# From the block loop to the tail: tile-by-tile loads through POOL's queue, a pool of its own for grad_out, the last products by kind and w_down in pieces

## The chip, the cores and the metric

The kernel runs on one core of one Trainium2 chip, as one launch. The time is device microseconds (us) of one execution; times are given as the median of several runs, and one execution was also taken by the profiler. Smaller is better.

## The reference

It is the forward pass and all gradients of a block with an adaptive layer norm, a spectral mixer and a bilinear feed-forward, for 2048 tokens (S), width 576 (D) and hidden width 4608 (F), in bfloat16.

```python
def A_ref(x, w_r, w_i):                       # spectral mixer
    X = jnp.fft.rfft2(x.astype(jnp.float32), axes=(-2, -1))
    return jnp.fft.irfft2(X * (w_r + 1j * w_i), s=(S, D), axes=(-2, -1)).astype(jnp.bfloat16)

def B_ref(x, w_gate, w_up, w_down):           # bilinear feed-forward
    return ((x @ w_gate) * (x @ w_up)) @ w_down

def f(x, w_r, w_i, w_gate, w_up, w_down, c, w_mod):
    sa, ca, ga, sb, cb, gb = split6(silu(c) @ w_mod)
    h = layernorm(x) * (1 + ca) + sa
    x = x + ga * A_ref(h, w_r, w_i)
    h = layernorm(x) * (1 + cb) + sb
    return x + gb * B_ref(h, w_gate, w_up, w_down)

out, vjp = jax.vjp(f, x, w_r, w_i, w_gate, w_up, w_down, c, w_mod)
return (out, *vjp(grad_out))                  # eight gradients
```

## The kernel before

The 2048 tokens are 16 tiles of 128, the hidden width is 36 blocks of 128 (`fb`). The Fourier transforms are matmuls with tables that lie in DRAM. The work goes in four stretches: a head (the forward mixer and the start of the gradient of the hidden layer), the loop over the 36 blocks, the backward mixer (`t1`, then `t2`), and the last products (`t3`), with the output `x + gb * B`.

**The block loop** computes, for each `fb`, gate and up (`gup`, L620 and L625), their products with the hidden gradient (`hhT`, `ggT`, `guT`), the sum of the gradient that goes back to the tokens (`u8p`, matmuls of L654, added into `acc` by DVE at L659), and three weight gradients (`product(fb, 0..2)`, matmuls `u57p` of L572): 0 is `gon` (grad_out) by `hh_sf`, 1 is `h2p` by `gg_sf` and 2 is `h2p` by `gu_sf`. The `_sf` tiles are the block's tiles with tokens on the partitions, made by DMA transposes on SP's queue (L643). Each product is two groups (halves of the width) of 16 matmuls of 128x288, stored through `so` and, for 1 and 2, turned once more by DMA (`woT`, L583) before the store. `hhT` of every block is also stored to DRAM (`hhT_d`, L638, POOL's queue), since `t3` needs it in another layout.

**From loop to tail.** Behind the last block come 32 `u8p` outputs of four matmuls each, which finish `acc` tile by tile, and six products: those of block 34 (0, 1, 2) and of block 35 (0, 1, 2). Beside them runs `t1`, sixteen tiles through four steps: `t1_norm` (DVE and ACT: the gradient of the second layer norm, `gn`, `jk`, `ab`, `u`, `v`, and with grad_out `gxr`, `gyr`; L850 to L861), `t1_turn` (PE transposes `trp` L866, and column sums by matmul: `csA` from n2c, `csB`, `csC` from yc; L769), `t1_cols` (`zp`, L886, table RD) and `t1_rows` (`vp`, L894, table G1, result `b_Vp`). `t1_norm` loads `n2c` (the normed tokens), `goc` (grad_out) and `yc` (the mixer's output) for two tiles at a time, from SP's queue, in two buffers each (L835); it stores `gxr` per tile from POOL's queue (L860).

**t2** works through 19 chunks of frequencies and takes `wn` (the spectral weights, L917, one DMA on POOL's queue). **t3** computes `u3p` (L1113): for each of 16 tiles and two halves of the width 36 matmuls, `hl` (hidden rows, four DMAs of 9 blocks for every two tiles, L1099) by `wdA` (w_down's blocks 0 to 14) and `wdB` (blocks 15 to 35), both loaded by SP (L1088). t3's matmuls fill PE beside t2. Five of its tiles start a `section` that finishes a gradient of the modulation (`pr`, L803).

**What sets the order.** A scheduler places the instructions of every engine in one fixed order by priorities: work in `tc.high_priority(n)` is placed as if it stood n earlier in the program. `HEAD_START` (350) and `SPREAD` (40) give t1 and t2 that lead; the six products are what is placed last, as fill. `tc.issue_after(x)` keeps an instruction behind x on the same engine's queue; `behind(list)` does it for several. A queue issues in order: an instruction that waits holds up all behind it. A tile's buffer comes free when the last reader of the tile that had it is done, and a pool that is opened where another has been closed waits tile by tile for what lies there. Before, `wdB`'s one buffer lies over `hh_sf`, `gg_sf` and `gu_sf` of both last blocks.

Of the kernel before, what the change touches and what calls it, by code (L numbers as in the profile page):

```python
# [19 lines left out]
NT = 16  # L20
# [10 lines left out]
NCH = 19  # L31
HEAD_START = 350
SPREAD = 40


def _tables():
# [46 lines left out]
def build(ctx, tc, A_x, A_w_r, A_w_i, B_w_gate, B_w_up, B_w_down, c_in, w_mod, grad_out,  # L83
# [93 lines left out]
    res3cm = tc.tile_pool(name="res3", bufs=1, reuse_waits="tile")  # L177
    res3 = res3cm.__enter__()
    h2T = res3.tile([128, NT, 5, 128], BF, name="h2T")
    res2cm = tc.tile_pool(name="res2", bufs=1, reuse_waits="tile")  # L180
    res2 = res2cm.__enter__()
    h2p = res2.tile([128, NT, DP], BF, name="h2p")
    h2n = h2p[:, :, 0:D]
    gonf = res2.tile([128, NT * D + 64], BF, name="gon")
    gon = gonf[:, 0:NT * D].rearrange("p (t d) -> p t d", t=NT)

    with ExitStack() as hs:
        def pool(name, bufs, side="left", space=None, stack=hs):
# [332 lines left out]
    with ExitStack() as ms:  # L521
# [13 lines left out]
        with ExitStack() as bs:  # L535
# [99 lines left out]
            def turn_items(fb):  # L635
                def turns_():
                    hhT, ggT, guT = trip[fb][2:5]
                    nc.gpsimd.dma_start(hhT_d[:, :, fb, :].rearrange("tp f x -> f tp x"), hhT[:].rearrange("f (tp ti) p -> f tp (ti p)", ti=2))  # L638
                    sfs[fb] = []
                    for nm, srcT in (("hh_sf", hhT), ("gg_sf", ggT), ("gu_sf", guT)):  # L640
                        sf = sfp.tile([128, NT, 128], BF, name=nm)
                        with tc.high_priority(-2 * HEAD_START if fb == NFB - 1 else 0):
                            turned = nc.sync.dma_start_transpose(out=sf[:], in_=srcT[:].rearrange("f t p -> f (t p)"))  # L643
                        sfs[fb].append(sf)
                    if fb % FBT == 1 and fb + 3 < NFB:
                        wTs[fb // FBT + 1] = wT_load(fb + 3, [turned.ins] * 5)
                return turns_
# [49 lines left out]
                for h in range(2):  # L697
                    u8_output([NFB - 2, NFB - 1], t, h)
            fill.clear()
            for fb_ in (NFB - 2, NFB - 1):  # L700
                for i in range(3):
                    for f in product(fb_, i):
                        f()
        res2cm.__exit__(None, None, None)
        res3cm.__exit__(None, None, None)

    with ExitStack() as ts:
# [11 lines left out]
        tl0 = pool("tl0", 1)  # L721
        o2p = pool("o2p", 2)
        oAp = pool("oAp", 1)
        oBp = pool("oBp", 1)
        tl = pool("tl", 1)
        Vp = pool("vp", 1).tile([128, NG, 128], BF, name="b_Vp")
        tl3 = pool("tl3", 1)
# [90 lines left out]
        with ExitStack() as r1:  # L818
# [6 lines left out]
            with tc.high_priority(HEAD_START):  # L825
                for k in rings:
                    nc.vector.memset(rings[k][:, :, D:DP], 0.0)
            ld, gyTs, zts = {"order": []}, {}, {}

            def t1_norm(t):  # L830
                if t % 2 == 0:
                    for k, src in (("n2c", n2_d), ("goc", go_v), ("yc", y_d)):
                        ld[k] = c1.tile([128, 2, D], BF, name=k)
                        with behind(ld["order"]):
                            ins = nc.sync.dma_start(ld[k][:], src[:, t:t + 2, :])  # L835
                        if t == 4:
                            ld["after"] = ins.ins
                    if t < 4:
                        ld["order"] = [ins.ins]
                        with behind(ld["order"]):  # L840
                            for k, tag in ((("RD", "tA"),), (("G1", "tB"), ("BD2", None), ("BDA", None)))[t // 2]:
                                T[k] = load_table(tl0, k, tag)
                        ld["order"] = [tab_ins[k]]
                    ld[t // 2] = (ld["n2c"], ld["yc"])
                n2 = ld["n2c"][:, t % 2, :]
                gh, gx, gy = (rings[k][:, t % 3, 0:D] for k in ("ghr", "gxr", "gyr"))
                nc.scalar.copy(gh, acc(t))
                s12 = c1.tile([128, 2], FP32, name="s12")
                gn = c1.tile([128, D], BF, name="gn2")
                nc.vector.scalar_tensor_tensor(out=gn[:], in0=acc(t), scalar=1.0, in1=opcb_h[:], op0=MUL, op1=MUL, accum_out=s12[:, 0:1])  # L850
                jk = c1.tile([128, D], BF, name="jk2", bufs=1)
                nc.vector.scalar_tensor_tensor(out=jk[:], in0=gn[:], scalar=1.0, in1=n2, op0=MUL, op1=MUL, accum_out=s12[:, 1:2])
                ab = c1.tile([128, 2], FP32, name="ab2")
                nc.vector.tensor_scalar(out=ab[:], in0=s12[:], scalar1=-1.0 / D, scalar2=rstd2g[:, t:t + 1], op0=MUL, op1=MUL)
                u = c1.tile([128, D], BF, name="u2")
                nc.scalar.activation(out=u[:], in_=gn[:], func=ACT.Identity, bias=ab[:, 0:1], scale=rstd2g[:, t:t + 1])
                v = c1.tile([128, D], BF, name="v2", bufs=1)
                nc.vector.scalar_tensor_tensor(out=v[:], in0=n2, scalar=ab[:, 1:2], in1=u[:], op0=MUL, op1=ADD)
                nc.vector.tensor_tensor(out=gx, in0=v[:], in1=ld["goc"][:, t % 2, :], op=ADD)
                nc.gpsimd.dma_start(gx1_d[:, t, :], gx)  # L860
                nc.vector.tensor_tensor(out=gy, in0=gx, in1=ga_h[:], op=MUL)  # L861

            def t1_turn(t):
                pt = ps_fp.tile([128, 5, 128], BF, name="trp", tag="fp")
                for m in range(5):
                    nc.tensor.transpose(pt[:, m, :], rings["gyr"][:, t % 3, wide(m)], ident[:])  # L866
                gyTs[t] = c1.tile([128, 5, 128], BF, name="gyT")
                nc.scalar.copy(gyTs[t][:], pt[:])
                gh, gx = rings["ghr"][:, t % 3, :], rings["gxr"][:, t % 3, :]
                n2c, yc = ld[t // 2]  # L870
                if t == 0:
                    add_zero(csA, csB, csC, first=True)
                for h in range(2):
                    colsum(csB, h, gh[:, h * 288:(h + 1) * 288])
                diag(csA, csB, 288, gh, n2c[:, t % 2, :])
                diag(csC, csB, 352, gx, yc[:, t % 2, :])
                if t == NT - 1:
                    add_zero(csA, csB, csC, first=False)

# [23 lines left out]
            after = ld["after"]  # L903
# [10 lines left out]
        rA = ts  # L914
        ra = pool("ra", 1, "right", stack=rA)
        wn = ra.tile([128, 2, NT, FP], BF, name="wn2")
        nc.gpsimd.dma_start(wn[:].rearrange("k c a f -> k (c a f)"), wn_d)  # L917
        fg = pool("fg", 2, "right", stack=rA)
        rB = ExitStack()
        A_ = pool("rb", 1, "right", stack=rB).tile([128, 2, NT, FP], BF, name="j_A")  # L920
# [160 lines left out]

        csF = ps_cs.tile([128, 512], FP32, name="csF", tag="csB")
        wdA = oAp.tile([128, 15, D], BF, name="wdA")
        wdB = oBp.tile([128, NFB - 15, D], BF, name="wdB")

        def wd_load(dst, k, f0, n):
            with tc.issue_after(after):
                nc.sync.dma_start(dst[:, k:k + n, :], B_w_down[f0 * 128:(f0 + n) * 128, :].rearrange("(j f) d -> f j d", f=128))  # L1088

        wd_load(wdA, 0, 0, 8)  # L1090
        wd_load(wdA, 8, 8, 7)
        prs = {}
        for tp_ in range(NT // 2):
            hls = []
            for b0 in range(0, NFB, 9):
                nq = 4 * tp_ + b0 // 9
                hl = hlp.tile([128, 9, 256], BF, name="hl2") if nq >= 12 and (nq - 12) % 13 < 7 else o2p.tile([128, 9, 256], BF, name="hl", bufs=6)
                with tc.issue_after(after):
                    nc.sync.dma_start(hl[:], hhT_d[tp_, :, b0:b0 + 9, :])  # L1099
                hls.append(hl)  # L1100
                if tp_ == 0 and b0 in (9, 18):
                    wd_load(wdB, 10 * (b0 // 9 - 1), 15 + 10 * (b0 // 9 - 1), 9 + b0 // 9)
            x1t = o2p.tile([128, 2, D], BF, name="x1t3", bufs=1)
            nc.gpsimd.dma_start(x1t[:], x1_d[:, 2 * tp_:2 * tp_ + 2, :])
            got = o2p.tile([128, 2, D], BF, name="got3", bufs=1)
# [1 line left out]
            for ti in range(2):  # L1107
                t = 2 * tp_ + ti
                ob = o2p.tile([128, D], BF, name="ob3")
                for h in range(2):  # L1110
                    p2 = ps_u3.tile([128, 512], FP32, name="u3p")
                    for fb in range(NFB):
                        mm = nc.tensor.matmul(p2[:, 0:288], lhsT=hls[fb // 9][:, fb % 9, ti * 128:(ti + 1) * 128], rhs=(wdA[:, fb] if fb < 15 else wdB[:, fb - 15])[:, h * 288:(h + 1) * 288], start=(fb == 0), stop=(fb == NFB - 1))  # L1113
# [99 lines left out]
```

## Time and profile before

| | |
|---|---|
| median of 3 runs | 1591.95 us (1589.98 to 1597.13) |
| profiled execution | 1594.8 us, of which span 1593.0 us |
| mean granted clock of PE | 0.992 |
| busy | PE 1535.0, DVE 1045.6, ACT 559.8, POOL 170.3 us |
| bytes moved by DMA | 280.64 MB, mean 176 GB/s |
| n2c, 288 KB, issue to landing | 4.6 us (median of eight) |
| gx_d, 144 KB, from POOL's queue | 3.3 us (median of sixteen) |
| wn, 2336 KB, from POOL's queue | 10.3 us |
| wdB, 1440 and 1584 KB, from SP's queue | 7.6 and 18.8 us |

An engine is busy when it executes. Its waits are put down to what came last. PE is TensorE's matmuls, DVE VectorE, ACT ScalarE, POOL GpSimd, SP SyncE; POOLq and SPq are their DMA queues. A line such as "PE csA L769 <- DMA n2c<-n_d: 2.4, 3, 1.3" reads: PE's instruction that writes csA at line 769 waited for the DMA that fills n2c from n_d, 2.4 us in all, three times, 1.3 us at the longest. A row of windows has the window, its length, and for PE, weight loads, DVE, ACT and POOL the busy time with the number of instructions; then the granted clock, the share of time in which the 16 DMA engines were busy, and GB/s. A row of the chain has its start, its length and what it was.

### The profile page before, as it was taken

What the parts mean: (1) busy time and instruction counts of PE and PEld (TensorE: products, weight loads), DVE (VectorE), ACT (ScalarE), POOL (GpSimd) and SP (SyncE); (2) the same over time, 40 slices, a digit from 0 to 9 for tenths busy, and PEclk for the clock granted to TensorE, in tenths of its full rate; (3) what the DMA queues carried; (4) which work ended last, traced back from release to release, by engine and by line L of the source; (5) the groups of instructions that cost most, each with busy time, mean ns of one, the idle gap of its engine ahead of it and who ended that gap; (6) DMA issues with size and microseconds to landing.
All of it is one profiled execution on the core that took longest, in us unless ns stands there. A gap on an engine that the chain in (4) does not pass through costs nothing.

```text
span 1593.0 us, 30039 instructions
## 1 busy us (share of the span) xinstructions
PE 1535.0 (96%) x11370; PEld 1035.0 (65%) x11370; DVE 1045.6 (66%) x2626; ACT 559.8 (35%) x1108; POOL 170.3 (11%) x283
## 2 busy tenths in 40 slices
PE   6999989999999999999999999999999989899997
PEld 4666533567666666766666676666666666677775
DVE  6866763666666666666666666666666774678655
ACT  6666632322222222222222222222222365466022
POOL 0001212101010100101010010101000011100232
PEclk9999999999999999999999999999999999999998
DMA  9869998779877686786868686767857786635775
GB/s 319 275 194 237 242 259 228 166 139 143 141 152 150 130 177 104 158 152 134 162 130 144 140 171 118 164 133 129 180 103 143 191 264 197 218 112 179 286 224 159
DMA packets 485252, 280.64 MB, mean 176 GB/s; under 512 B 407633, under 2 KB 452434, under 8 KB 484210
## 3 DMA queue, kind: packets, MB, share of 16 engines
q1 hardware_dynamic: 459922, 185.65, 55.1%
q0 software_dynamic: 25184, 93.07, 19.8%
q8 instruction: 89, 1.46, 0.4%
q14 instruction: 57, 0.47, 0.1%
HBM read 108.77 MB, written 82.31 MB: 120 GB/s over the span
## 4 chain that ended last, share of the span: by engine, by line
PE 77%; DMA 9%; DVE 7%; issue 3%; ACT 2%; SPq 0%; POOL 0%; DVEq 0%; ACTq 0%; POOLq 0%
PE u57p L572 26%; PE u8p L654 17%; PE gup L625 16%; PE u4p L377 7%; PE gup L620 2%; DMA xc<-in_A_x_dram 2%; DMA n2c<-n_d 2%; DMA Xn<-xn_d 2%; DMA wmj<-in_w_mod_dram 1%; DMA wdB<-in_B_w_down_dram 1%; DVE pr L803 1%; PE u3p L1113 1%; PE yp L485 1%; PE yp L1022 1%; PE zp L315 1%
## 5 line engine op out<-in xcount | busy, mean ns | idle before, releaser
L659 DVE TENSOR_TENSOR acc<-acc,u8p 128x288 f32<-128x288 f32 x1088 | 489.2, 454 | 314.6 <-PE u8p L654 314.2
L654 PE MATMUL u8p<-wT,ggT 128*128 128x288 bf16 x1152 | 327.5, 286 | 2.1 <-DVE acc L659 2.1
L654 PE MATMUL u8p<-wT,guT 128*128 128x288 bf16 x1152 | 327.2, 286 | 0.0
L625 PE MATMUL gup<-h2T,wgu 128*128 128x512 bf16 x1152 | 294.9, 379 | 0.0
L575 ACT CAST so<-u57p 128x288 bf16<-128x288 f32 x216 | 86.0, 398 | 521.4 <-PE u57p L572 515.6
L572 PE MATMUL u57p<-gon,hh_sf 128*128 128x288 bf16 x1152 | 188.6, 286 | 0.4 <-DMA hh_sf<-hhT 0.4
L572 PE MATMUL u57p<-h2p,gg_sf 128*128 128x288 bf16 x1152 | 187.6, 286 | 0.0
L572 PE MATMUL u57p<-h2p,gu_sf 128*128 128x288 bf16 x1152 | 186.2, 286 | 0.0
L625 PEld LDWEIGHTS <-wgu 128*128 128x128 bf16 x1152 | 109.5, 98 | 98.8 <-issue 17.1
L654 PEld LDWEIGHTS <-ggT 128*128 128x128 bf16 x1152 | 112.6, 98 | 67.2 <-issue 14.0
L377 PE MATMUL u4p<-goT,wdT 128*128 128x512 bf16 x656 | 151.1, 379 | 4.4 <-DVE ghh_st L141 3.8
L654 PEld LDWEIGHTS <-guT 128*128 128x128 bf16 x1152 | 112.7, 98 | 56.2 <-issue 2.6
L1113 PEld LDWEIGHTS <-hl 128*128 128x128 bf16 x1152 | 111.5, 98 | 35.7 <-issue 7.5
L572 PEld LDWEIGHTS <-hh_sf 128*128 128x128 bf16 x1152 | 112.6, 98 | 29.0 <-DMA hh_sf<-hhT 0.7
L572 PEld LDWEIGHTS <-gu_sf 128*128 128x128 bf16 x1152 | 112.5, 98 | 28.4
L572 PEld LDWEIGHTS <-gg_sf 128*128 128x128 bf16 x1152 | 112.5, 98 | 28.3
L627 ACT CAST gT<-gup 128x512 bf16<-128x512 f32 x144 | 84.3, 585 | 130.4 <-PE gup L625 130.4
L377 PEld LDWEIGHTS <-wdT 128*128 128x128 bf16 x656 | 61.9, 98 | 77.2 <-issue 11.5
L627 ACT CAST uT<-gup 128x512 bf16<-128x512 f32 x144 | 84.3, 585 | 73.6 <-PE gup L625 73.6
L1113 PE MATMUL u3p<-wdB,hl 128*128 128x288 bf16 x672 | 94.8, 288 | 8.0 <-DMA wdB<-in_B_w_down_dram 7.0
L638 POOL DMA_DIRECT2D hhT_d<-hhT x36 | 33.2, 921 | 504.4 <-DVE hhT L629 475.4
L139 ACT CAST ghh_st<-u4p 128x512 bf16<-128x512 f32 x88 | 51.1, 585 | 68.1 <-PE u4p L377 67.7
(358 smaller groups left out, 1734.0 us busy)
## 6 DMA issues: line engine op xcount, KB each, us to landing
ghhT_d<-ghh_st POOLq DMA_DIRECT2D x36, 512.0 KB, 4.7
ghh<-ghhT_d POOLq DMA_DIRECT2D x36, 512.0 KB, 7.3
hhT_d<-hhT POOLq DMA_DIRECT2D x36, 512.0 KB, 6.6
hl<-hhT_d SPq DMA_DIRECT2D x32, 576.0 KB, 6.9
out_dram<-woT SPq DMA_DIRECT2D x72, 128.0 KB, 2.0
wdn<-in_B_w_down_dram SPq DMA_DIRECT2D x18, 288.0 KB, 4.3
out_dram<-so SPq DMA_DIRECT2D x36, 144.0 KB, 2.6
wgu<-in_B_w_gate_dram SPq DMA_DIRECT2D x18, 256.0 KB, 3.4
```

The source lines that it names most:

```text
L139: nc.scalar.copy(dst, src)
L315: mm = nc.tensor.matmul(zp[:, :FP], lhsT=hTs[t][:, m, :], rhs=T["RD"][:, m, cc, :], start=(m == 0), stop=(m == 4))
L377: nc.tensor.matmul(pt[:], lhsT=wdTs[k][:, j, m, :], rhs=goT[:, 4 * sb4:4 * sb4 + 4, m, :], start=(m == 0 and n == 5), stop=(m == n - 1))
L572: mm = nc.tensor.matmul(pw[0][:, 0:288], lhsT=sf[:, t, :], rhs=rhs_n[:, t, h * 288:(h + 1) * 288], start=(t == 0), stop=(t == NT - 1))
L575: nc.scalar.copy(so[:, h * 288:(h + 1) * 288], pw[0][:, 0:288])
L620: nc.tensor.matmul(pts[-1][:], lhsT=wgu[r, 8, jw * 128:(jw + 1) * 128], rhs=h2T[r, 4 * sb4:4 * sb4 + 4, 4, :], start=True, stop=False)
L625: nc.tensor.matmul(pts[k][:], lhsT=wgu[:, 4 * wi_ + m, jw * 128:(jw + 1) * 128], rhs=h2T[:, ts_, m, :], start=False, stop=(m == 3))
L627: nc.scalar.copy((gT, uT)[wi_][:, ts_, :], pts[k][:])
L638: nc.gpsimd.dma_start(hhT_d[:, :, fb, :].rearrange("tp f x -> f tp x"), hhT[:].rearrange("f (tp ti) p -> f tp (ti p)", ti=2))
L654: nc.tensor.matmul(pu[:, 0:288], lhsT=l_, rhs=r_, start=(k == 0), stop=(k == len(mms) - 1))
L659: nc.vector.tensor_tensor(out=dst, in0=dst, in1=pu[:, 0:288], op=ADD)
L1113: mm = nc.tensor.matmul(p2[:, 0:288], lhsT=hls[fb // 9][:, fb % 9, ti * 128:(ti + 1) * 128], rhs=(wdA[:, fb] if fb < 15 else wdB[:, fb - 1 ...
```

## The change

1. **grad_out in its own pool.** `gon` and `h2p` lay in one pool, `gon` above `h2p`. Now `gon` has a pool of its own below `h2p`'s, and each is given up by itself.
2. **Last products by kind.** The six run as 0 of 34, 0 of 35, 1 of 34, 1 of 35, 2 of 34, 2 of 35. The transpose that makes `hh_sf` of block 35 is no longer put late with the other two.
3. **t1's loads by tile.** `n2c`, `goc` and `yc` come one tile at a time (147,456 bytes instead of 294,912, the 288 KB of the profile's rows), in four buffers instead of two of double size, through POOL's queue instead of SP's. The chain that held them and the tables in one order is gone; the tables are asked for with tiles 0 and 1.
4. **wn in four pieces** on POOL's queue, behind the gx stores of tiles 7, 9, 11 and 13.
5. **w_down in pieces.** `wdA` comes in four DMAs on POOL's queue, behind the yc loads of tiles 4, 6, 8 and 10, instead of two on SP's. `wdB` becomes three pools of seven blocks, each loaded by two DMAs on SP's queue, between the first four `hl`. Those `hl` and the first four wdB pieces get the priority `AHEAD` (3000); `hl` is no longer held behind t1's loads.

```diff
+AHEAD = 3000
...
-    res2 = res2cm.__enter__()
-    h2p = res2.tile([128, NT, DP], BF, name="h2p")
-    gonf = res2.tile([128, NT * D + 64], BF, name="gon")
+    res2gcm = tc.tile_pool(name="res2g", bufs=1, reuse_waits="tile")
+    gonf = res2gcm.__enter__().tile([128, NT * D + 64], BF, name="gon")
+    res2cm = tc.tile_pool(name="res2", bufs=1, reuse_waits="tile")
+    h2p = res2cm.__enter__().tile([128, NT, DP], BF, name="h2p")
...
-                        with tc.high_priority(-2 * HEAD_START if fb == NFB - 1 else 0):
+                        with tc.high_priority(-2 * HEAD_START if fb == NFB - 1 and nm != "hh_sf" else 0):
...
-            for fb_ in (NFB - 2, NFB - 1):
-                for i in range(3):
+            for i in range(3):
+                for fb_ in (NFB - 2, NFB - 1):
                     for f in product(fb_, i):
                         f()
...
-        oBp = pool("oBp", 1)
+        oBps = [pool("oB%d" % k, 1) for k in range(3)]
...
-                if t % 2 == 0:
-                    for k, src in (("n2c", n2_d), ("goc", go_v), ("yc", y_d)):
-                        ld[k] = c1.tile([128, 2, D], BF, name=k)
-                        with behind(ld["order"]):
-                            ins = nc.sync.dma_start(ld[k][:], src[:, t:t + 2, :])
...
+                for k, src in (("n2c", n2_d), ("goc", go_v), ("yc", y_d)):
+                    ld[k] = c1.tile([128, D], BF, name=k, bufs=4)
+                    ins = nc.gpsimd.dma_start(ld[k][:], src[:, t, :])
+                ld["at", t] = ins.ins
+                for k, tag in {0: (("RD", "tA"),), 1: (("G1", "tB"), ("BD2", None), ("BDA", None))}.get(t, ()):
+                    with tc.issue_after(tab_ins["RD"]) if t else ExitStack():
+                        T[k] = load_table(tl0, k, tag)
...
-        nc.gpsimd.dma_start(wn[:].rearrange("k c a f -> k (c a f)"), wn_d)
+        for k in range(4):
+            with tc.issue_after(ld["gx", 7 + 2 * k]):
+                nc.gpsimd.dma_start(wn[:, k // 2, 8 * (k % 2):8 * (k % 2) + 8, :].rearrange("k a f -> k (a f)"), wn_d[:, k * 8 * FP:(k + 1) * 8 * FP])
...
-        wdB = oBp.tile([128, NFB - 15, D], BF, name="wdB")
-        wd_load(wdA, 0, 0, 8)
-        wd_load(wdA, 8, 8, 7)
+        wdBs = [oBps[k].tile([128, 7, D], BF, name="wdB%d" % k) for k in range(3)]
+        def wd_load(f0, n, t):
+            dst = wdA[:, f0:f0 + n, :] if f0 < 15 else wdBs[(f0 - 15) // 7][:, (f0 - 15) % 7:(f0 - 15) % 7 + n, :]
+            with tc.issue_after(ld["at", t]) if t < NT else ExitStack():
+                (nc.gpsimd if t < NT else nc.sync).dma_start(dst, B_w_down[f0 * 128:(f0 + n) * 128, :].rearrange("(j f) d -> f j d", f=128))
+        for k in range(4):
+            wd_load(4 * k, 3 if k == 3 else 4, 4 + 2 * k)
...
-                with tc.issue_after(after):
+                with tc.high_priority(AHEAD if tp_ == 0 else 0):
                     nc.sync.dma_start(hl[:], hhT_d[tp_, :, b0:b0 + 9, :])
...
-                if tp_ == 0 and b0 in (9, 18):
-                    wd_load(wdB, 10 * (b0 // 9 - 1), 15 + 10 * (b0 // 9 - 1), 9 + b0 // 9)
+                if tp_ == 0 and b0 < 27:
+                    f0 = 15 + 7 * (b0 // 9)
+                    with tc.high_priority(AHEAD if b0 < 18 else 0):
+                        wd_load(f0, 4, NT)
+                        wd_load(f0 + 4, 3, NT)
```

More of the change, by code (lines that the diff above doesn't have):

```diff
@@ L704, in build @@
         res2cm.__exit__(None, None, None)
+        res2gcm.__exit__(None, None, None)
         res3cm.__exit__(None, None, None)
@@ L827, in build @@
                     nc.vector.memset(rings[k][:, :, D:DP], 0.0)
-            ld, gyTs, zts = {"order": []}, {}, {}
+            ld, gyTs, zts = {}, {}, {}
             def t1_norm(t):
-                if t % 2 == 0:
-                    for k, src in (("n2c", n2_d), ("goc", go_v), ("yc", y_d)):
-                        ld[k] = c1.tile([128, 2, D], BF, name=k)
-                        with behind(ld["order"]):
-                            ins = nc.sync.dma_start(ld[k][:], src[:, t:t + 2, :])
[L836 to L845, printed above, removed]
+                for k, src in (("n2c", n2_d), ("goc", go_v), ("yc", y_d)):
+                    ld[k] = c1.tile([128, D], BF, name=k, bufs=4)
+                    ins = nc.gpsimd.dma_start(ld[k][:], src[:, t, :])
+                ld["at", t] = ins.ins
+                ld[t] = (ld["n2c"], ld["yc"])
+                for k, tag in {0: (("RD", "tA"),), 1: (("G1", "tB"), ("BD2", None), ("BDA", None))}.get(t, ()):
+                    with tc.issue_after(tab_ins["RD"]) if t else ExitStack():
+                        T[k] = load_table(tl0, k, tag)
+                n2 = ld["n2c"][:]
                 gh, gx, gy = (rings[k][:, t % 3, 0:D] for k in ("ghr", "gxr", "gyr"))
@@ L858, in t1_norm @@
                 nc.vector.scalar_tensor_tensor(out=v[:], in0=n2, scalar=ab[:, 1:2], in1=u[:], op0=MUL, op1=ADD)
-                nc.vector.tensor_tensor(out=gx, in0=v[:], in1=ld["goc"][:, t % 2, :], op=ADD)
-                nc.gpsimd.dma_start(gx1_d[:, t, :], gx)
+                nc.vector.tensor_tensor(out=gx, in0=v[:], in1=ld["goc"][:], op=ADD)
+                ld["gx", t] = nc.gpsimd.dma_start(gx1_d[:, t, :], gx).ins
                 nc.vector.tensor_tensor(out=gy, in0=gx, in1=ga_h[:], op=MUL)
@@ L869, in t1_turn @@
                 gh, gx = rings["ghr"][:, t % 3, :], rings["gxr"][:, t % 3, :]
-                n2c, yc = ld[t // 2]
+                n2c, yc = ld[t]
                 if t == 0:
@@ L874, in t1_turn @@
                     colsum(csB, h, gh[:, h * 288:(h + 1) * 288])
-                diag(csA, csB, 288, gh, n2c[:, t % 2, :])
-                diag(csC, csB, 352, gx, yc[:, t % 2, :])
+                diag(csA, csB, 288, gh, n2c[:])
+                diag(csC, csB, 352, gx, yc[:])
                 if t == NT - 1:
@@ L902, in build @@
                             steps[s_](k - s_)
-            after = ld["after"]
             dcb = diag_rows(tl, csA, csB, 288, "dcb")
@@ L1083, in build @@
         wdA = oAp.tile([128, 15, D], BF, name="wdA")
-        wdB = oBp.tile([128, NFB - 15, D], BF, name="wdB")
-        def wd_load(dst, k, f0, n):
-            with tc.issue_after(after):
-                nc.sync.dma_start(dst[:, k:k + n, :], B_w_down[f0 * 128:(f0 + n) * 128, :].rearrange("(j f) d -> f j d", f=128))
-        wd_load(wdA, 0, 0, 8)
-        wd_load(wdA, 8, 8, 7)
+        wdBs = [oBps[k].tile([128, 7, D], BF, name="wdB%d" % k) for k in range(3)]
+        wds = [wdA[:, fb] if fb < 15 else wdBs[(fb - 15) // 7][:, (fb - 15) % 7] for fb in range(NFB)]
+        def wd_load(f0, n, t):
[4 more added lines that the diff above has]
+            wd_load(4 * k, 3 if k == 3 else 4, 4 + 2 * k)
         prs = {}
@@ L1097, in build @@
                 hl = hlp.tile([128, 9, 256], BF, name="hl2") if nq >= 12 and (nq - 12) % 13 < 7 else o2p.tile([128, 9, 256], BF, name="hl", bufs=6)
-                with tc.issue_after(after):
+                with tc.high_priority(AHEAD if tp_ == 0 else 0):
                     nc.sync.dma_start(hl[:], hhT_d[tp_, :, b0:b0 + 9, :])
                 hls.append(hl)
-                if tp_ == 0 and b0 in (9, 18):
-                    wd_load(wdB, 10 * (b0 // 9 - 1), 15 + 10 * (b0 // 9 - 1), 9 + b0 // 9)
+                if tp_ == 0 and b0 < 27:
[3 more added lines that the diff above has]
+                        wd_load(f0 + 4, 3, NT)
             x1t = o2p.tile([128, 2, D], BF, name="x1t3", bufs=1)
@@ L1112, in build @@
                     for fb in range(NFB):
-                        mm = nc.tensor.matmul(p2[:, 0:288], lhsT=hls[fb // 9][:, fb % 9, ti * 128:(ti + 1) * 128], rhs=(wdA[:, fb] if fb < 15 else wdB[:, fb - 15])[:, h * 288:(h + 1) * 288], start=(fb == 0), stop=(fb == NFB - 1))
+                        mm = nc.tensor.matmul(p2[:, 0:288], lhsT=hls[fb // 9][:, fb % 9, ti * 128:(ti + 1) * 128], rhs=wds[fb][:, h * 288:(h + 1) * 288], start=(fb == 0), stop=(fb == NFB - 1))
                     nc.scalar.copy(ob[:, h * 288:(h + 1) * 288], p2[:, 0:288])
```

## The prediction

> **What bounds the kernel now.** I read the page's busy shares first, then the table of windows over the stretch that the diff touches (1245 to 1370 us), then PE's waits there, the chain that ended last and SP's own timeline.
>
> ```profile
> PE 1535.0 (96%) x11370; PEld 1035.0 (65%) x11370; DVE 1045.6 (66%) x2626; ACT 559.8 (35%) x1108; POOL 170.3 (11%) x283
> ```
>
> PE is the bound. It idles 58 us in the whole span, so a change that takes no matmul away can bring only what PE stands still in its own stretch. The windows (PEclk, DMA share and GB/s at the end of the line) tell where:
>
> ```profile
> 1253.90:1256.00 2.10, 0.23 (x2) 0.10 (x1) 1.30 (x4) 0.00 (x0) 0.00 (x0) 1.00 1.02 419
> 1276.00:1300.00 24.00, 21.00 (x209) 16.28 (x208) 17.49 (x46) 17.64 (x36) 2.80 (x6) 1.00 0.96 302
> 1300.00:1306.00 6.00, 1.62 (x17) 1.38 (x15) 1.88 (x6) 1.43 (x3) 0.43 (x1) 0.87 1.13 299
> 1306.00:1338.00 32.00, 31.57 (x290) 23.75 (x288) 21.70 (x55) 19.73 (x40) 6.48 (x12) 0.97 0.49 140
> 1350.00:1366.00 16.00, 7.99 (x78) 5.80 (x78) 6.33 (x18) 4.30 (x9) 1.31 (x3) 0.89 1.04 396
> 1366.00:1370.00 4.00, 4.00 (x30) 3.23 (x28) 1.68 (x5) 1.69 (x4) 0.00 (x0) 0.58 0.35 143
> 1370.00:1400.00 30.00, 29.59 (x314) 21.71 (x312) 24.34 (x73) 18.06 (x37) 3.86 (x7) 1.00 0.47 152
> ```
>
> PE is idle 1.9, 3.0, 4.4 and 8.0 us in four of them, and the DMA share is about 1 each time; behind two of the gaps the clock is low (0.97 over 32 us, 0.58 over 4 us). PE's waits of 1253 to 1257, 1276 to 1300, 1300 to 1306 and 1338 to 1366 name what came last:
>
> ```profile
> PE u8p L654 <- DVE acc L659: 1.9, 1, 1.9
> ...
> PE csA L769 <- DMA n2c<-n_d: 2.4, 3, 1.3
> ...
> PE csA L769 <- DMA n2c<-n_d: 4.4, 1, 4.4
> ...
> PE u3p L1113 <- DMA wdB<-in_B_w_down_dram: 7.0, 2, 5.6
> PE u3p L1113 <- DMA hl<-hhT_d: 1.0, 1, 1.0
> ```
>
> The first is an n2c wait too: `acc` stands on DVE behind `jk`, and DVE waited 1.9 us for n2c there. The chain shows the lengths of these transfers:
>
> ```profile
> 1247.17 7.44 DMA n2c<-n_d
> ...
> 1278.02 3.05 DMA n2c<-n_d
> ...
> 1297.86 7.09 DMA n2c<-n_d
> ...
> 1346.57 18.78 DMA wdB<-in_B_w_down_dram
> ```
>
> The same 288 KB (0.295 MB) take 3.05 us or 7.09 us: the slow one has the 2.4 MB `wn` (issued 1293.00) beside it. The last wdB piece leaves SP 8.8 us after the last product (which ends at 1337.79; I call this end P) and lands at P+27.6. Behind 1370 PE is 99% busy, until 1578.
>
> **The change, part by part.** The sum stands against the profiled run, 1594.8 us (span 1593.0 and 1.8 around it); that is 2.9 us above the median 1591.95, and I shift the result by that.
>
> *First load.* n2c of tile 0 now has half the bytes and goes through POOL, behind the hhT_d store of block 35 (issued 1247.05, 0.90 us). It landed at 1254.6; with 0.9 us of store issue, 0.54 us of its own (row of the gx_d issues) and the landing of hhT_d in this stretch (6.0 us) as the slower bound, of gx_d (144 KB, median 3.3) as the faster, it lands between 1251.9 and 1254.5. I take 1253.1: gain 1.4 us of the 1.9 (0 to 1.9).
>
> *The other loads.* 24 SP issues go, 48 of 144 KB come on POOL, and with four wdA and three more wn pieces POOL issues 55 x 0.54 = 30 us more; it is busy 16 of the 125 us now, so its time is free, but its order isn't. In the changed program's order goc of tile t+4 waits for gx of tile t on DVE, and behind it stand n2c of tile t+5, yc, and the pieces of wdA and wn. n2c waits for v on DVE and for the csA matmul of the tile four before. Buffers hold the same four tiles, so a request goes no earlier in tiles, only in smaller steps. I walked the DVE, POOL and PE orders with 0.54 us an issue, 3.3 us of landing (gx_d, min/median/max 2.0/3.3/6.9) and DVE's 3.3 us a tile: seven loads still come late, by 1.4 (tile 4), 1.7 (5), 1.2 (9), 0.5 (yc 10), 1.3 (12), 0.9 (14) and 1.3 us (15), 8.3 in all, as against 8.4 us of jk waits before. Some 1.4 us of these lie under products on PE, so PE keeps 6.9 us of waits for its 7.3 (7.0 for n2c, 0.3 for gxr), and saves some 0.7 us of slow clock that the one long wait cost (ten zp matmuls took 2.10 us behind it, 1.40 elsewhere). Gain 1.1 us. Bounds: with the shortest landing, 2.0, five of the seven go, 0.5 us is left on the other two, and 7 us are gained; with 4 us, 0.7 more on each is a loss of about 4.
>
> A page would have this otherwise: the Trainium skill, "DMA: Bandwidth & Descriptors", section Anatomy of one DMA, fits 2.0 us plus bytes over 436 GB/s for a POOL-issued DMA, which is an estimate of 2.3 us here, near the shortest gx_d row and below the median; by it this term would be a gain of some 6 us, and the sum 5 us better.
>
> *wn and wdA in pieces on POOL.* Now one of 2.4 MB and two of 1.0 and 1.1 MB push n2c aside; eight of 0.6 MB do it by 1.5 us each (0.59 MB at 396 GB/s). That is in the lateness of tiles 5 to 15 above. Nobody waits for wn or wdA before P: wdA's first use is 3.7 us behind it, and its last piece goes around tile 11.
>
> *wdB and hl.* In the changed order SP issues hl0 and the first wdB piece some 4 us before P; hl1 to hl3 and the next pieces wait for the slots that the last products read, and go at P to P+2.5; the last two at about P+4.5 and behind hl3's landing. Ahead of the last use lie 2.36 MB of hl, 3.1 of wdB, 0.9 of T_IR and 1.6 of T_GB, 7.9 MB: at the 396 GB/s of the 1350 window 20 us, from P-4 on, so until about P+17. PE reaches the last piece after 18.6 us of matmul behind P (0.122 us each, from 13 u3p in 1.59 us). It just fits; before it landed at P+27.6. Gone are 8.0 us of waits and 4.0 x 0.42 = 1.7 us of slow clock, 9.7. Left I put 1.7: 0.6 us for dcb, dga and dsb, which now come behind fm inside t2 and on which the csD and csE zero matmuls wait, and 1.1 us for hl1, which PE needs 8.5 us behind P. Gain 8.0 (5, if transfers run at the 302 GB/s of the 1276 window; 9.7 at most).
>
> *At nothing:* `gon` in its own pool and the products by kind only decide which slot is free first; the same 192 matmuls run as fill. hh_sf of block 35 turns earlier on SP, where gu_sf, gg_sf and the tables now follow it; its first reader was never waited for in this stretch. If that cover failed, the transposes' 5 us row would be the price.
>
> Sum: 1.4 + 1.1 + 8.0 = 10.5 us. PE's stream behind 1370 has no gap that could take it back, and the sections' chain at the end is started by u3 tiles, so it moves along. 1594.8 - 10.5 = 1584.3 for the profiled run, 1581.5 on the median's scale. Own range: gains of 1 to 17 us, 1575 to 1591.
>
> **The rivals.** *A, every stall goes:* landing at the 2.0 us end. 1.9 + 7 + 9.7 = 18.6 us, so 1573.4. For it: 1306 to 1338, where transfers were few (DMA share 0.49), had almost no PE wait. Against: the chained order on POOL.
>
> *B, wdB doesn't start early:* SP's queue is in order, and hl0 stands behind the store chain of the gradients; if hl1 keeps the rest until P+6, as the first wdB piece does now (1343.72), only the t1 terms are left and the pieces' finer steps: 2.5 us, 1589.5. For it: the hl rows sat 10.8 us on SP in the old order. Against: the priorities put them ahead of the last woT.
>
> *C, slower: POOL's queue is the new wait.* Place: n2c and goc through one in-order queue with the next load behind the last gx. If they land in 6.0 us (the hhT_d row of this queue in this stretch) and not 3.3, each of the seven late loads costs 2.7 us more, 18.9 in all: 18.9 - 10.5 = 8.4 us slower, 1600.4. It decides from 4.8 us of landing on (10.5 over 7 is 1.5 more). For it: the longest gx_d landing, 6.9. Against: sixteen issues of gx_d took 540 to 564 ns with DVE 73% busy, and their median landing was 3.3. Beside it stands a rule against this change: the Trainium skill, "SBUF — State Buffer", section SBUF: two separate sides, says that while DVE runs an operation in a two-port mode GpSimd can't write the descriptors of a DMA issued from POOL, and advises SP or ACT instead. Its example goes from 0.62 to 3.1 us; an estimate by it, 2.5 us more on each of seven, is 7 us slower than before. The even gx_d issues speak against it, though the landing of a load among jk, gn and v is shown by no row.
>
> **How the numbers follow.** Forecast 0.55, A 0.15, B 0.15, C 0.15. About 0.5% (8 us) is what a measurement of this kernel tells from no change. Faster: A, and 0.43 of the forecast's 0.55: 0.58. Same: the other 0.12, B, and 0.02 of C: 0.29. Slower: 0.13. The range reaches from A to between the median and C: 1573 to 1596.
>
> **What would show it.** Right: no gap over 2 us between 1276 and 1306; clock 1.0 from 1306 to 1370; u3p's wait for wdB under 2 us, with hl0 issued before the last product. Wrong: n2c rows on POOL's queue landing above 4.8 us; DVE waiting for n2c more than 8.4 us in all; csA's waits for n2c above 7.3; a wait of u3p for hl; PE below 99% behind 1370.

## The result and the profile after

The changed kernel takes 1601.97 us (median of 11 runs, 1594.9 to 1607.81), the kernel before beside it 1592.55 (11 runs, 1589.98 to 1597.45): a ratio of 1.0053, 95% interval [1.0037, 1.0068]. The medians are 9.4 us apart, to the slower side, where 10.5 us of gain were forecast. The profiled execution took 1601.68 us, span 1599.8.

PE does the same work (1539.0 us busy, 1535.0 before). First the windows of the stretch, cut as before (window, its length, busy PE, weight loads, DVE, ACT, POOL, then clock, DMA share, GB/s):

```profile
1245.30:1253.90 8.60, 7.34 (x58) 5.51 (x57) 6.05 (x17) 0.00 (x0) 4.65 (x8) 1.00 1.19 150
1253.90:1256.00 2.10, 0.00 (x0) 0.00 (x0) 0.00 (x0) 0.00 (x0) 0.00 (x0) 1.00 0.98 88
1256.00:1276.00 20.00, 14.23 (x96) 10.49 (x96) 13.11 (x36) 4.89 (x8) 2.67 (x5) 0.74 1.12 210
...
1300.00:1306.00 6.00, 5.26 (x53) 4.02 (x51) 5.39 (x14) 4.58 (x10) 3.61 (x7) 1.00 0.97 292
...
1366.00:1370.00 4.00, 1.65 (x14) 1.30 (x14) 2.35 (x8) 0.69 (x2) 0.00 (x0) 0.93 1.06 395
```

The gap of 4.4 us at 1300 is gone, as the change meant, and most of the 8.0 behind the last product (3.1 are left, at 1366). But PE now stands still from 1252.6 to about 1261.7, at a DMA share near 1 and at first only 88 GB/s. Behind the gap the clock is low: 0.74 is its mean from 1256 to 1276, and by windows of 4 us it reads 0.60 (no matmul runs there), 0.50, 0.62 and then 1.00. PE's waits from 1240 to 1400 name it:

```profile
PE u8p L655 <- DVE acc L660: 9.1, 1, 9.1
PE csA L771 <- DMA n2c<-n_d: 6.1, 6, 2.1
PE u3p L1115 <- DMA wdB<-in_B_w_down_dram: 3.1, 1, 3.1
PE trp L862 <- DVE gyr L857: 1.3, 1, 1.3
```

The first row was 1.9 us before. DVE itself waited 9.2 us for n2c of tile 0, with `acc` behind `jk` in its order. What moved at that time is in SP's and POOL's timelines (start, length of the issue) and in the DMA rows of 1244 to 1280 (median us to landing):

```profile
1245.04 4.76 SPq L644 DMA_TRANSPOSE hh_sf<-hhT  x1
...
1254.74 13.42 SPq L644 DMA_TRANSPOSE gu_sf<-guT  x1
1268.26 8.61 SPq L644 DMA_TRANSPOSE gg_sf<-ggT  x1
```

```profile
1245.31 0.90 POOL L639 DMA_DIRECT2D hhT_d<-hhT  x1 [23.45 <-DVE hhT L630]
1246.20 2.17 POOL L835 DMA_DIRECT2D n2c<-n_d  x4
```

```profile
n2c<-n_d POOLq DMA_DIRECT2D x4, 144.0 KB, 14.9
...
hhT_d<-hhT POOLq DMA_DIRECT2D x1, 512.0 KB, 14.8
...
hh_sf<-hhT SPq DMA_TRANSPOSE x1, 15.9
gu_sf<-guT SPq DMA_TRANSPOSE x1, 22.7
gg_sf<-ggT SPq DMA_TRANSPOSE x1, 12.2
```

Before, the three transposes landed in 5.0, 4.7 and 5.9 us and the hhT_d store in 6.2. Now the store and the n2c loads beside them take 14 to 17 us, and the transposes two to five times as long as before. Everything behind slides: the last product ends at 1345.99 instead of 1337.79.

The packets of the queues say what moved (packets, MB, the time that they took as a share of the 16 engines' time; q1 is SP's queue, q0 POOL's). First the changed kernel from 1250 to 1254, then the kernel before from 1263 to 1270, where hh_sf and gg_sf move with nothing from POOL's queue beside them:

```profile
q1 hardware_dynamic: 491, 0.13, 94.5%
q0 software_dynamic: 37, 0.14, 34.4%
```

```profile
q1 hardware_dynamic: 4008, 1.02, 89.2%
```

In both, nearly all of SP's packets are a transpose's, of some 256 bytes. One took 25 ns before (0.892 x 16 x 7 us / 4008) and 123 ns in the changed kernel (0.945 x 16 x 4 us / 491), where POOL's loads got 0.14 MB through in 4 us. The tables T_RD and T_G, which also come earlier now, are not what moved then: from 1248 to 1256 SP's queue moved 0.41 MB in 1590 packets, so hardly anything but transposes.

**Two lengths.** The head's end moves from one execution to the next: the hhT_d store of block 35 (S) is issued at 1238.7 to 1249.3 in the profiles of this study, which is more than most of what is compared. So each profile is read by two lengths as well: S to the end of the last product (P), and P to the end (E).

| kernel | ratio [95%] | S to P | P to E | u8p wait | wdB + hl wait |
|---|---|---|---|---|---|
| before | 1 | 90.7 | 255.2 | 2.1 | 8.0 |
| before, second profile | | 90.3 | 256.3 | 1.1 | 8.2 |
| changed | 1.0053 [1.0037, 1.0068] | 100.7 | 253.8 | 9.1 | 3.1 |
| e1_hh_late | 1.0030 [1.0003, 1.0057] | 99.0 | 251.7 | 4.0 | 3.2 |
| e3_hh_early_alone | 1.0027 [1.0001, 1.0053] | 97.5 | 254.6 | 5.6 | 6.4 |
| e4_tail_alone | 0.9988 [0.9965, 1.0010] | 90.9 | 254.0 | 2.5 | 3.2 |
| e5_loads_alone | 1.0001 [0.9974, 1.0028] | 94.5 | 255.7 | 4.6 | 7.9 |
| e6_wdb2_ahead | 1.0017 [0.9997, 1.0037] | 89.6 | 262.3 | 2.8 | 6.0 |
| e7_first_sp | 0.9991 [0.9969, 1.0012] | 90.3 | 251.7 | 0.9 | 3.8 |
| e8_store_sp | 1.0017 [0.9994, 1.0039] | 102.3 | 250.4 | 9.7 | 3.0 |
| e9_all_sp | 0.9998 [0.9978, 1.0019] | 94.2 | 254.6 | 1.3 | 3.2 |
| e10_tables_late | 0.9934 [0.9906, 0.9962] | 93.3 | 247.9 | 0.9 | 0.0 |
| e11_five_n2c | 0.9965 [0.9943, 0.9988] | 93.9 | 247.6 | 2.5 | 0.0 |
| e12_first_act | 1.0060 [1.0036, 1.0084] | 103.7 | 254.8 | 9.5 | 3.8 |

(us; one profile each. In e8 the store is on SP's queue, and S is taken 0.90 us ahead of the first n2c load, where it stands in the changed kernel. The u8p wait is that of the stretch's first 30 us. In e9 and e11 the profiled execution is the slowest of its kernel.) By these the change costs 9.9 us up to P and gives 1.4 us back behind it, 8.5 in all, against 9.4 between the medians. Two profiles of the kernel before differ by 0.4 and 1.1 us. But e7 and e10, which are one program up to P, differ by 3.0 there, so under 3 us the table alone shows nothing.

### The profile page after: what moved, and what is told of

Its sections match the earlier page's. It is cut to its first block, busy times and chain, and to the rows that moved or that the text cites. A ratio compares the mean times of both kernels' runs of the same rounds, so it can differ in the third digit from the quotient of the medians.

```text
span 1599.8 us, 30100 instructions
## 1 busy us (share of the span) xinstructions
PE 1539.0 (96%) x11370; PEld 1034.4 (65%) x11370; DVE 1045.4 (65%) x2626; ACT 559.4 (35%) x1108; POOL 200.4 (13%) x338
## 4 chain that ended last, share of the span: by engine, by line
PE 77%; DMA 9%; DVE 6%; issue 5%; ACT 2%; SPq 1%; POOL 0%; DVEq 0%; POOLq 0%; ACTq 0%
PE u57p L573 26%; PE u8p L655 17%; PE gup L626 15%; PE u4p L378 8%; PE gup L621 2%; DMA Xn<-xn_d 2%; DMA gu_sf<-guT 1%; DMA wmj<-in_w_mod_dram 1%; DMA n2c<-n_d 1%; PE yp L486 1%; DVE pr L805 1%; DMA xc<-in_A_x_dram 1%; DMA wdB<-in_B_w_down_dram 1%; PE zp L316 1%; DVE gwt L931 1%
```

## The experiments

Theory 1: the transposes of block 35, moving beside the first loads, hold n2c of tile 0 back. Theory 2: POOL's queue is slow for these loads whatever moves beside it.

**e1: hh_sf late again.** The changed kernel with

```diff
-                        with tc.high_priority(-2 * HEAD_START if fb == NFB - 1 and nm != "hh_sf" else 0):
+                        with tc.high_priority(-2 * HEAD_START if fb == NFB - 1 else 0):
```

> The changed kernel with one condition undone: the transpose that makes hh_sf of block 35 is put late again with the other two, so that SP issues T_RD, T_G and the small tables first and the three transposes behind them. Theory 1 (the transposes of block 35 move beside the first POOL loads and hold n2c of tile 0 back, 16.7 us from issue to landing): n2c of tile 0 lands in under 9 us, the u8p wait falls from 9.1 to under 2.5 us and the low clock behind it (0.60, 0.50, 0.62 in three windows of 4 us, 2.6 us of loss) goes: 9 to 10 us below the changed kernel, about 1592, ratio to before 1.000. Theory 2 (POOL's queue is slow for these loads whatever stands beside it): no change, about 1602, ratio 1.006, u8p still waits some 9 us.

Between the two. The u8p wait fell from 9.1 to 4.0 us, not under 2.5, and n2c of tile 0 landed after 9.2 us (14.3 in the changed kernel, whose 16.7 is tile 3's). With the loads gone from SP's queue, nothing held the late transposes back, and gg_sf took hh_sf's place in the order:

```profile
1244.29 11.28 SPq L644 DMA_TRANSPOSE gg_sf<-ggT  x1
1255.61 5.07 SPq L644 DMA_TRANSPOSE hh_sf<-hhT  x1
1260.72 3.05 SPq L644 DMA_TRANSPOSE gu_sf<-guT  x1
```

But gg_sf is not what moves beside the first loads here. Packets from 1246 to 1250:

```profile
DMA packets 139, 1.34 MB, mean 335 GB/s; under 512 B 4, under 2 KB 4, under 8 KB 44
q1 hardware_dynamic: 101, 1.17, 86.3%
q0 software_dynamic: 37, 0.15, 9.6%
```

SP's queue moves 1.17 MB in 101 packets, all but four of them large: T_G, issued at 1242.39, and the end of T_RD, and no transpose. POOL's queue gets 0.15 MB through. So the wait that is left in e1 lies beside the tables, which part 3 of the change no longer keeps behind the first loads.

And hh_sf, which the product order by kind now asks for second, was waited for on PE (2.6 us, none before). Undoing the condition undoes neither the product order nor the early tables.

**e3: hh_sf early alone,** the same condition put into the kernel before.

> The kernel before with that one condition alone: hh_sf of block 35 is turned right behind gu_sf, ahead of n2c, which still comes through SP's own queue in pieces of two tiles. Theory 1: one more transpose of some 5 us ahead of n2c in the same queue makes the u8p wait 1.9 + 5 = 7 us, and about 1.5 us of slow clock follow: 6 us slower than before, ratio 1.004. If transposes cost the loads only across two queues: under 1 us, ratio 1.000. Theory 2: ratio 1.000.

5.6 us of u8p wait, S to P 6.8 us longer and a ratio of 1.0027: a little under theory 1's price (7 us, 1.004) for one transpose ahead in the same queue, with all loads on SP. (hh_sf itself took 9.5 us there, issued 0.09 us behind POOL's hhT_d store and 1.4 us behind gu_sf on its own queue.)

**e4 and e5: the two halves of the change.** e4 is the kernel before with the tail's part (`gon`'s pool, products by kind, wdB in pieces, AHEAD), e5 the kernel before with the loads' part (tile by tile on POOL, wn and wdA in pieces); hh_sf late in both.

> The kernel before with only the tail's part: grad_out in its own pool, the last products by kind, wdB in three pools and six pieces, hl and wdB ahead by priority; t1's loads, wn, wdA and the late hh_sf as before. If the wdB term was right in kind: u3p's waits for wdB and hl fall from 8.0 to about 3 us (3.1 in the changed kernel) and the low clock behind them to under 1 us, 5 us faster, 1587.5, ratio 0.997. The rival, that PE only waits elsewhere (n2c in t1, the new dcb, dga and dsb waits, n1c in t2): under 2 us, ratio 0.999 or more.

> The kernel before with only the loads' part: n2c, goc and yc tile by tile in four buffers on POOL's queue, wn and wdA in pieces on POOL's queue; one pool, product order, wdB, hl and the late hh_sf as before. Theory 1: without the early transpose the loads are no worse than before, ratio 0.999 to 1.001, n2c of tile 0 landing under 9 us. Theory 2: 8 us slower, ratio 1.005, with n2c of tile 0 landing in more than 12 us.

e4: the waits fell as the first theory has it, from 8.0 to 3.2 us, but the time only by a ratio of 0.9988, whose interval holds 1. e5: level by its ratio (its median is 2.6 us higher), with S to P 3.8 us longer in its profile; n2c of tile 0 landed after 9.7 us (expected: under 9), with the tables ahead of it on SP as in e1, and gg_sf after 16.9. Neither half alone is 9 us slower; theory 2 with 8 us is out.

**e8: is it the store ahead of n2c in POOL's queue?** The changed kernel with

```diff
-                    nc.gpsimd.dma_start(hhT_d[:, :, fb, :]...
+                    (nc.sync if fb == NFB - 1 else nc.gpsimd).dma_start(hhT_d[:, :, fb, :]...
```

> The changed kernel, hh_sf early, with one transfer moved: the store of hhT_d of block 35 goes through SP's queue, just ahead of the hh_sf transpose, so that on POOL's queue nothing stands ahead of n2c of tile 0. If that store (14.8 us to land in the changed kernel, 6.0 before) is what held n2c back in the queue: n2c of tile 0 lands in under 7 us, u8p waits under 2 us instead of 9.1, and the stretch from the end of the loop to the last product shortens by 7 us or more. If the transposes slow whatever moves beside them: n2c lands in 9 us or more, u8p waits 4 us or more.

No, though tile 0's load did land in 6.6 us: with the store gone from POOL's queue it is issued 24 us earlier, at 1215.5, while the loop still runs. DVE then waits 9.7 us for tile 1's load, issued at 1239.55 with nothing ahead of it on POOL's queue, and that one lands after 16.1 us (the slowest of the changed kernel: 16.7). hh_sf and gu_sf take 18.6 and 20.4, and u8p waits 9.7. The ratio is below the changed kernel's all the same (1.0017); S to P is longer, so what is gained lies behind P (250.4) or ahead of S, and why stays open.

**e12: is it POOL's queue?** The changed kernel with

```diff
-                    ins = nc.gpsimd.dma_start(ld[k][:], src[:, t, :])
+                    ins = (nc.scalar if t < 4 else nc.gpsimd).dma_start(ld[k][:], src[:, t, :])
```

> The changed kernel, hh_sf early, with the loads of tiles 0 to 3 on ACT's queue instead of POOL's; SP's order is untouched. It asks whether the slow transposes and loads come from POOL's queue or from any second queue beside the transposes. If any second queue does it: hh_sf and gu_sf of block 35 still land in over 12 us, n2c of tile 0 in over 9, u8p waits over 4 us. If it is POOL's queue: transposes in 5 to 9 us, n2c of tile 0 under 7 us, u8p under 2.5 us.

No again. DMA rows of its 1244 to 1280:

```profile
n2c<-n_d ACTq DMA_DIRECT2D x4, 144.0 KB, 14.7
...
hh_sf<-hhT SPq DMA_TRANSPOSE x1, 17.6
gu_sf<-guT SPq DMA_TRANSPOSE x1, 4.6
gg_sf<-ggT SPq DMA_TRANSPOSE x1, 4.9
```

Tile 0's load left 1.2 us ahead of hh_sf and landed in 3.6 us. The next three left from 1246.9 on, behind hh_sf's start at 1246.47, and took 14.0 to 15.7, from ACT's queue as from POOL's; hh_sf beside them took 17.6, and DVE's long wait is now for tile 1. gu_sf and gg_sf, issued at 1269.05 and 1271.15 when nearly all loads were through, take 4.6 and 4.9, against over 12 for gu_sf by the first reading: they met little. The Trainium skill, "DMA: Bandwidth & Descriptors", section Issuing engines are not separate DMA queues, says that transfers of all issuing engines interleave on the same 16 DMA engines; the runs agree in that the queue's name made no difference.

**e7 and e9: keep them apart.** e7 is e1 with the loads of tiles 0 to 3 back on SP, in the old order (chained, tables between), so that the queue itself puts the transposes behind them; tiles 4 to 15 stay on POOL. e9 has all sixteen tiles' loads and wdA on SP.

```diff
+                    with behind(ld["order"] if t < 3 else []):
+                        ins = (nc.sync if t < 4 else nc.gpsimd).dma_start(ld[k][:], src[:, t, :])
...
+                for k, tag in {1: (("RD", "tA"),), 2: (("G1", "tB"), ("BD2", None), ("BDA", None))}.get(t, ()):
```

> The changed kernel with hh_sf late again and with the loads of tiles 0 to 3 on SP's queue, ahead of the tables and of the transposes hh_sf and gg_sf, as the kernel before orders them; tiles 4 to 15 stay on POOL's queue, wn and wdA too. Theory 1 (block 35's transposes and POOL's first transfers, moving together, are what costs; 8 us of the 99 between the store of hhT_d of block 35 and the last product): the stretch goes back from 98.95 to about 91 us (before: 90.7), the transposes land in about 5 us and u8p waits about 2 us. Theory 2 (POOL's queue for tiles 4 to 15 costs as well): the stretch stays above 94 us. Ratio to before: 0.998 by theory 1, 1.001 or more by theory 2.

> As e7_first_sp, but the loads of all sixteen tiles and wdA's pieces go through SP's queue; tile by tile in four buffers, wn in pieces on POOL's queue. It tells POOL's queue from the four small buffers. If POOL's queue costs tiles 4 to 15 anything (its order of goc behind gx, wdA pieces ahead of n2c): csA's and jk's waits for n2c fall and the stretch is over 2 us shorter than in e7. If not: within 1 us of e7, or longer, since the loads then stand behind SP's stores that wait for products.

e7 is what theory 1 expects: u8p 0.9 us, hh_sf and gg_sf 5.7 and 5.4, S to P 90.3, ratio 0.9991. It puts the tables and the two transposes behind the first loads together, so it doesn't divide the cost between them. POOL's queue for tiles 4 to 15 costs nothing that shows: e9 has 7.3 us of csA waits for n2c, e7 6.9, a median landing of 3.9 against 4.0, and S to P 3.9 us longer than e7's. That also bears on the rule that spoke against the change (the Trainium skill, "SBUF — State Buffer", section SBUF: two separate sides: while DVE runs in a two-port mode, POOL can't write descriptors): beside a busy DVE these loads landed no later from POOL than from SP. No view says in which mode DVE ran here.

**e6 and e10: what is left in the tail.** e6 is e4 with the third wdB pool's pieces ahead of the last woT transpose on SP; e10 is e7 with two tables held back.

```diff
-                    with tc.high_priority(AHEAD if b0 < 18 else 0):
+                    with tc.high_priority(AHEAD if b0 < 18 else AHEAD // 2):
```

```diff
-        T["GB"] = load_table(tl0, "GB", "tB", nc.gpsimd)
-        T["IR"] = load_table(tl0, "IR", "tA", nc.gpsimd)
+        for k, tag in (("GB", "tB"), ("IR", "tA")):
+            with tc.issue_after(ld["xn", 12]):
+                T[k] = load_table(tl0, k, tag, nc.gpsimd)
```

> The tail's part alone, as in e4_tail_alone, and one priority more: the two pieces of the third wdB pool get AHEAD // 2, which puts them on SP's queue in front of the last woT transpose and of opca_h instead of behind them. If the wait that was left in e4 (u3p for wdB, 3.2 us, some 25 us behind the last product, and slow clock behind it) is SP's order: it falls under 1 us, and the time from the last product to the end goes from 254.0 to about 251 us; ratio to before 0.997. The rival, that the DMA engines are full there (share 1.0 to 1.1) and the order doesn't matter: the wait stays near 3 us or moves to hl, 254 us, ratio 0.999.

> e7_first_sp with one edit: the tables T_IR and T_GB (2.4 MB, in e7 issued 10 us behind the last product and first read 60 us later) go on POOL's queue behind the Xn load of t2's fourth filter step. If the transfers that stand beside wdB are what left a wait in the tail (3.8 us in e7, DMA share 1.0 to 1.1 from 10 to 20 us behind the last product): u3p's wait for wdB goes to under 1 us and the time from the last product to the end falls from 251.7 to about 248 us, ratio to before 0.997. The rival, that SP's own order of wdB behind the last woT transpose and opca_h holds the last two pieces: the wait stays at 3 us or more and the ratio at 0.999.

In e6 the wait grew, and one that the forecast had put at 0.6 us came beside it:

```profile
PE u3p L1120 <- DMA wdB<-in_B_w_down_dram: 6.0, 1, 6.0
PE csD L761 <- DVE dcb L776: 5.4, 1, 5.4
```

dcb waits for the woT transpose that wdB had been put in front of: issued at 1338.1, it landed only at about 1367, with wdB, hl and both tables beside it. The order alone is not it. e10 takes bytes away, and the wait goes, though the last two wdB pieces leave no earlier (P+8.3 and P+15.2; e7: P+8.2 and P+15.3). Windows from P on, ten us each, first e7, then e10:

```profile
1346.80:1356.80 10.00, 8.63 (x85) 6.22 (x84) 6.11 (x17) 4.72 (x10) 3.53 (x10) 1.00 1.11 333
1356.80:1366.80 10.00, 7.08 (x44) 4.52 (x44) 3.65 (x12) 1.90 (x5) 0.00 (x0) 0.66 0.69 263
```

```profile
1344.50:1354.50 10.00, 9.70 (x97) 7.06 (x96) 6.09 (x17) 4.91 (x11) 2.56 (x8) 1.00 1.07 268
1354.50:1364.50 10.00, 9.05 (x91) 6.55 (x89) 8.15 (x25) 4.24 (x10) 0.57 (x1) 1.00 0.24 96
```

In the second window of each pair the DMA share falls from 0.69 to 0.24 and the clock holds. T_GB is issued at 1365.2 in e10 and first read at 1402.4: it never had to move beside wdB. e10 is 0.9934 [0.9906, 0.9962] of the kernel before, 1583.42 us against 1591.79, and so beats both kernels. Its profile doesn't show all of that as a gain of its edits: of the 10.6 us between its span and that of the kernel before, 7.3 lie behind P, S to P is 2.6 longer, and 5.9 lie ahead of S, by about as much as two profiles of the kernel before differ there (5.3).

**e11: five buffers for n2c** (three for goc), on top of e10.

```diff
-                    ld[k] = c1.tile([128, D], BF, name=k, bufs=4)
+                    ld[k] = c1.tile([128, D], BF, name=k, bufs={"n2c": 5, "goc": 3, "yc": 4}[k])
```

> e10_tables_late with five buffers for n2c and three for goc (yc keeps four; the bytes are the same). If the late n2c loads of t1 come from the distance of four tiles, as the prediction's walk has it: csA's and jk's waits for n2c (6.9 us on PE in e7) fall by a third or more, the stretch from the hhT_d store to the last product by 2 us. The rival, that the queue behind gx and the DMA engines set them: waits within 1 us of e10's, and goc's third buffer may cost DVE waits of its own.

PE's waits for n2c vanish (5.4 to 0.0), and jk's fall from 8.6 to 4.6, so the distance did set them, but others take their place (csC for gxr 4.4, hh_sf 2.3, yc 0.8) and S to P is 93.9 against 93.3: nothing gained.

**The kernel before again.**

> The kernel before once more, for a second profile: how far the time from the store of hhT_d of block 35 to the last product (90.7 us) and from there to the end (255.2) move between two executions of one kernel. Within 1 us each, if these two lengths are what kernels may be compared by.

90.3 and 256.3 us; 1590.22 us. The second length moved by 1.1, a little over what was expected.

## Why the prediction was wrong, by its steps

**"At nothing"** is the step that failed. It saw that hh_sf turns earlier on SP, with gu_sf, gg_sf and the tables behind it, asked only who waits for hh_sf, and left it at a 5 us transpose. It didn't ask what moves beside it: hh_sf took 15.9 us, and the first loads with it. **"First load"** listed what stands ahead of n2c on its own queue (the store, 6.0 us at the worst; its row says 6.2) and found 1251.9 to 1254.5. DVE got it at 1260.6. That the tables no longer stood behind the first loads was not weighed either; e1 shows a wait beside them (4.0 us, before 2.1). Instead of 1.4 us gained, u8p's wait went from 1.9 to 9.1, 7.2 us lost, and the clock behind that gap cost more work: three windows of 4 us from 1256 on have 0.60, 0.50 and 0.62, which is 2.23 x 0.50 + 4.00 x 0.38 = 2.6 us of PE's work. Together 9.8, where S to P grew by 9.9; smaller terms go both ways (0.9 less for n2c and some 1.2 less slow clock behind 1300, 1.3 more for gyr and 0.5 for acc). e8 and e12 show that it needs neither the store ahead on the loads' queue nor POOL's queue. The packets show that transposes moved in that gap, not tables. e7 shows that it goes when the tables and two of the three transposes stand behind the loads.

**"The other loads"** held in size: csA kept 6.1 us of n2c waits (6.9 forecast, 7.0 before), and 6.9 in e7. The median landing was 3.9 us, by the forecast's bounds (3.3, 4.0) a small loss rather than 1.1 us of gain; such a difference is below what the lengths show. With the first load's wait, DVE stood 15.7 us for n2c in all, past the 8.4 that the forecast had named as a sign of being wrong.

**"wdB and hl"** was right in kind and mis-sized: 8.0 us forecast. P to E is 253.8, and over the seven profiles with the new tail and the tables T_IR and T_GB as they were (changed, e1, e4, e7, e8, e9, e12) 253.0 on average (e6 and the two with those tables late left out), against 255.5 over the four with the old one (before twice, e3, e5): 2.5 us. So even without the loss ahead of P the 10.5 us would not have come: e7 is at 0.9991. hl0 left SP 4.1 us ahead of P, as forecast. The last two wdB pieces left at P+9.4 and P+15.1, not at P+4.5 and a little later, since the woT transpose and opca_h stood ahead. And the 20 us that the forecast itself had worked out for 7.9 MB gave no room for that; it "just fits" only if nothing slips. In that sum stood the 2.5 MB of T_IR and T_GB, and when those are first read was not asked; e10 shows that with them out of the way the late pieces cost nothing. Of the 9.7 us of waits and slow clock before, 3.1 us of waits are left, and the slow clock: 0.93 and 0.95 in the last two windows from 1366 to 1400 cost 1.65 x 0.07 + 29.45 x 0.05 = 1.6 us. Two waits that the kernel before did not have in its first profile take more back later: csD for n1c 1.7 us and u3p for ob 1.8. 9.7 - 4.7 - 3.5 = 1.5, about the 1.4 of the profile. The n1c wait was there in the second profile of before too (1.7), so how much of it is the change's stays open.

**The rivals.** C forecast a slower kernel by another way: seven late loads at 6.0 us of landing. That did not come (3.9), so that its 1600.4 lies near the measured 1601.97 is luck. B had SP's order hold wdB back; hl0 and the first piece did leave early, the last two pieces did not, and e6 and e10 show that the order alone was not the limit. No rival had a transpose and a load slow each other.

**Open:** why they do. The DMA share reads about 1 while 88 to 150 GB/s move, because each packet takes longer; whether that comes of the transposes' many small packets or of how the queues take turns, no run here separates. It isn't always so: in the kernel before, from 1248 to 1250, gu_sf moved 1227 packets at 22 ns each (0.836 x 16 x 2 us / 1227) beside the hhT_d store. No run has hh_sf early, the first loads on another queue and the tables late, so what the tables and the transposes each cost there is told apart by the packets alone. And e5, with transposes and loads meeting as well, is level by its ratio though its S to P is 4 us longer.

## What to carry to other kernels

When a load is moved to another queue, look not only at what stands ahead of it there, but at what the old queue kept it apart from: SP's order had held the tables and two of the three transposes behind the first loads, and nothing in the code said what that was worth. Before pieces are cut finer or put earlier, list what else moves in that window and when it is first read: holding back 2.4 MB of tables that nobody read for 60 us took 3.8 us off P to E (e7 to e10), the pieces and priorities 2.5. Where the head of a run moves by more than the effect, compare lengths between two fixed instructions, and take a second profile of the same kernel to learn what such a length is worth.

## What was not expected of the hardware

A DMA transpose of 512 KB that lands in 4.6 to 5.9 us with little beside it (the kernel before, e7, e12) took 15.9 to 18.6 as hh_sf in the changed kernel, e12 and e8, with 1.0 to 1.5 MB of plain transfers from other queues beside it; loads of 144 KB beside it took 14.0 to 16.7 us instead of the median 3.9. The issue on SP is held up too (13.42 us for gu_sf, 1.34 before). One plain store of 512 KB, with a load behind it, does less: in the loop of the kernel before, hh_sf landed after 7.5 to 10.5 us in seven blocks where the hhT_d store was issued up to 4 us ahead of it, and after 4.5 to 7.0 us in six where it was issued 7 us or more ahead.
